# Moving the first weight block's operands beside the attention, with a fifth row buffer and earlier scores

## The chip, the cores and the metric

The kernel runs on one core of one Trainium2 chip. The metric is the time of one execution in device microseconds (us). The engines are named as the profile names them: PE (TensorE; PEld is its weight load), DVE (VectorE), ACT (ScalarE), POOL (GpSimd) and SP (SyncE, which here only issues DMAs).

## The reference

Two layers in float32. First a "talking heads" attention over 4 batches, 12 heads, 448 positions and 64 values per head: the heads are mixed with a 12x12 matrix before the softmax and with another after it. Then a gated layer on the 1792 rows of 768 values that come out.

```python
scores = scale * np.matmul(q, k.transpose(0, 1, 3, 2))
scores = np.einsum('bhij,hg->bgij', scores, w_pre)
scores = scores - np.max(scores, axis=-1, keepdims=True)
attn = np.exp(scores)
attn = attn / (np.sum(attn, axis=-1, keepdims=True) + 1e-09)
attn = np.einsum('bhij,hg->bgij', attn, w_post)
x = np.matmul(attn, v)          # then (1792, 768)
gate = 1.0 / (1.0 + np.exp(-(x @ w_gate)))
val = x @ w_val
return gate * val @ w_out       # w_gate, w_val (768, 1536), w_out (1536, 768)
```

## The kernel before, in words

**Attention.** The 448 query rows of a batch are cut into blocks of 120, 120, 120 and 88 rows, 16 blocks in all. A block is cut into units of twenty rows (two sets of ten; the last unit of a batch has one set): 6, 6, 6 and 5 units, 92 units in all (`NU`). One pass of the main loop is a slot `s`. In it stand, for different units, the steps of a software pipeline: `scores` (q times k for two heads, then `keep` copies both to the staging tile `st`, one copy on ACT and one on DVE), `regroup` (SP's DMA from `st` to a row buffer `T`, issued `LEAD` = 6 slots ahead of the slot that bears the unit's number, into `T` buffer u mod 4), `premix` (PE, three slots ahead, into three PSUM banks `pm` used in turn), `rowmax` (DVE, line 219), `expo` (ACT, 226), `norm` and `scale` (DVE reciprocal 232, POOL 238: `ph`, the high half of the probabilities), `p_lo` (DVE 244: the low half), `postmix` (PE 256), `mix` (ACT 264) and `av` (PE 285: times v, one block later; ACT evicts it, 293). The single tile of `postmix` is read by `mix` before the next `postmix` may write it.

**The gated layer.** Weights and x are held as a pair of f16 halves: `round` (ACT, 1147) makes the high half, `rest` (DVE, 1152) the low one. A product of 2x2 blocks is done with seven products instead of eight, so each block of weights (`w` 0 to 5) and each half of x (`x` 0 and 1) needs seven operand pairs, P1, P2, P6, P5, P7, P4, P3, made from four quarters and four sums or differences of them (DVE `tt`, 1161). A product step (`gate`, PE 1168) is 18 matmuls of 128x448. The first steps are P1 and P2 of `w` 0, P1 and P2 of `w` 1, then the other five of `w` 0. `out_mm` (1179) is the last layer.

**What sets the order.** The attention's order is the code of the loop and the table `plan`. The work of the gated layer is a list of tasks that a planner (`order_tasks`) sorts at build time by due times (`DUE`), by how long ahead a buffer may be taken (`AHEAD`, `LEAVE`) and by when room comes free (`ROOM`). `moe.slot` issues what the plan has up to a set of the attention: from 15 sets before its end on, that is from unit 84, `until` puts those tasks at the end of a slot, or, in the last seven slots, ahead of the slot's own `expo` and `p_lo`. So `w` 0's rounds, rests and sums stand on ACT and DVE among the last units and behind them. Eight weight tiles are converted earlier, beside the attention (`early`), in scratch space `raws`; the largest values of v, needed for x's scale, are summed by `v_sum` (ACT 179).

Of the kernel before, what the change touches and what calls it, by code (L numbers as in the profile page):

```python
# [41 lines left out]
def _attention(ctx, tc, ins, B, H, S, D, xs, raws, make_moe):  # L42
# [151 lines left out]
    t_bufs = [tp.tile([128, 2, S], F32, name=f"T{i}") for i in range(4)]  # L194
# [79 lines left out]
    def av(bi, c):  # L274
# [133 lines left out]
    for s in range(min(min(plan), -LEAD), max(plan) + 1):  # L408
# [43 lines left out]
        tail = (av, moe.between, moe.early)  # L452
# [19 lines left out]
        for fn, args in todo:  # L472
            if fn in tail:
# [27 lines left out]
class _Moe:  # L501
# [23 lines left out]
    DUE = {('raw', 2): -12.8, ('bound', 'w', 2): 72.0, ('w', 2): 20.3, ('raw', 3): -44.5, ('bound', 'w', 3): 106.5,  # L525
# [3 lines left out]
        ('store', 0): -57.0, ('keep_h', 0): -7.8, ('sum_of', 0): 125.4, ('sigmoid', 0): 22.8, ('hidden', 0): -7.6,  # L529
        ('copy', 0): -5.8, ('sum', 0): 54.2, ('load_x', 0): -59.0, 'raws': (120.6, 11.4), 'pairs': (127.3, 180.1)}  # L530
    ROOM = ((-15, dict(B=9, A=8)), (-7, dict(B=2, A=2, T=3)), (0, dict(B=3, A=5)), (9.6, dict(B=5, A=8, T=7, R=0)))
    AHEAD = {'raw': 194.1, 'half': 900.0, 'w': 900.0, 's': 95.9, 't': 99.5, 'wp': 900.0, 'wq': 8.0, 'q': 11.2, 'qp': 15.0,
        'c': 900.0, 'snap': 613.6, 'tmp': 686.1, 'wide': 95.9, 'hq': 157.8, 'hqp': 900.0, 'ow': 900.0, 'os': 33.0, 'owp': 39.1}

    def __init__(self, tc, xs, ins, out, raws, NG, top):
# [383 lines left out]
    def group(self, t):  # L919
# [9 lines left out]
        if t.fn in (self.load_w, self.round, self.rest, self.tt, self.keep_pair):  # L929
# [209 lines left out]
    def scales(self, by, n):  # L1139
        up = self.one[("up",) + by[1:]]  # L1140
        e = up.shape[1]
        return [(up[:, i:i + 1], slice(i * n // e, (i + 1) * n // e)) for i in range(e)]

    def round(self, pair, f, by):
        hi, f = self.f16(pair)[0], self.f32(f)
        for up, part in self.scales(by, f.shape[1]):
            self.nc.scalar.activation(out=hi[:, part], in_=f[:, part], func=AF.Copy, scale=up)  # L1147

    def rest(self, pair, f, by):
        (hi, lo), f = self.f16(pair), self.f32(f)  # L1150
        for up, part in self.scales(by, f.shape[1]):
# [162 lines left out]
```

## Time and profile before

| what | value |
|---|---|
| runs | 786.03, 786.04, 789.07 us; median 786.04 us |
| profiled execution, its own time | 784.43 us |
| its span, first to last instruction | 782.6 us |
| busy, share of span | PE 97%, DVE 81%, ACT 73%, POOL 33% |
| mean granted TensorE clock | 0.995 |

Busy shares are averages over two stages with different limits. Matmuls are pipelined and their ends are modelled, so the share of PE hides short waits. The attention stage lasts to about 340 us, the gated layer from about 342 us to the end. A duration in a row reaches past the start of the next instruction by some hundredths of a microsecond.

### The profile page before, as it was taken

What the parts mean: (1) busy time and instruction counts of PE and PEld (TensorE: products, weight loads), DVE (VectorE), ACT (ScalarE), POOL (GpSimd) and SP (SyncE); (2) the same over time, 40 slices, a digit from 0 to 9 for tenths busy, and PEclk for the clock granted to TensorE, in tenths of its full rate; (3) what the DMA queues carried; (4) which work ended last, traced back from release to release, by engine and by line L of the source; (5) the groups of instructions that cost most, each with busy time, mean ns of one, the idle gap of its engine ahead of it and who ended that gap; (6) DMA issues with size and microseconds to landing.
All of it is one profiled execution on the core that took longest, in us unless ns stands there. A gap on an engine that the chain in (4) does not pass through costs nothing.

```text
span 782.6 us, 23675 instructions
## 1 busy us (share of the span) xinstructions
PE 762.2 (97%) x9623; PEld 423.2 (54%) x9623; DVE 631.7 (81%) x1089; ACT 569.2 (73%) x1138; POOL 261.9 (33%) x429
## 2 busy tenths in 40 slices
PE   8999999999999999889999999999999999999998
PEld 2465666566556666564555555555555555555554
DVE  4988899889888998879997988588777999996111
ACT  4898999999899999876876876587756784562000
POOL 2564547454734455520322312234222221010000
PEclk9999999999999999989999999999999999999999
DMA  6786678758885574719407294654577788994001
GB/s 194 251 267 226 199 249 264 256 172 255 256 265 193 188 239 169 250 55 318 149 29 254 67 323 157 242 204 153 187 216 267 282 297 311 388 376 179 36 36 70
DMA packets 81117, 166.17 MB, mean 212 GB/s; under 512 B 20720, under 2 KB 58192, under 8 KB 81008
## 3 DMA queue, kind: packets, MB, share of 16 engines
q1 hardware_dynamic: 73006, 133.14, 51.7%
q0 software_dynamic: 7728, 31.27, 10.3%
q8 instruction: 75, 1.23, 0.7%
q14 instruction: 34, 0.28, 0.1%
q10 hardware_dynamic: 274, 0.25, 0.1%
HBM read 87.77 MB, written 38.15 MB: 161 GB/s over the span
## 4 chain that ended last, share of the span: by engine, by line
PE 83%; ACT 6%; DMA 5%; DVE 3%; issue 1%; POOL 1%; SPq 0%; ACTq 0%; DVEq 0%; POOLq 0%
PE bank L1168 34%; PE bank L1179 18%; PE pm L214 9%; PE av L285 8%; PE qk L160 7%; PE mx L256 6%; DMA T<-st 2%; ACT e L226 2%; ACT mix L264 1%; ACT m L1147 1%; DVE m L1152 1%; DMA q<-in_qp_dram 1%; ACT st L166 1%; DVE pl L244 1%; DMA m<-w 1%
## 5 line engine op out<-in xcount | busy, mean ns | idle before, releaser
L1168 PEld LDWEIGHTS <-m 128*128 128x128 f16 x1512 | 147.7, 98 | 140.1 <-DVE m L1152 2.1
L1168 PE MATMUL bank<-m,m 128*128 128x448 f16 x1116 | 214.2, 352 | 1.7 <-DVE m L1152 1.7
L238 POOL TENSOR_SCALAR ph<-e,ss 128x448 f16<-128x448 f32 x180 | 116.1, 654 | 142.6 <-DVE ss L232 97.9
L226 ACT ACTIVATE e<-pm,nm 128x448 f32<-128x448 f32 x177 | 113.5, 642 | 25.8 <-DVE nm L219 23.1
L219 DVE TENSOR_REDUCE nm<-pm 128x1 f32<-128x448 f32 x177 | 101.7, 615 | 27.4 <-PE pm L214 23.7
L244 DVE SCALAR_TENSOR_TENSOR pl<-e,ss,ph 128x448 f16<-128x448 f32 x180 | 115.6, 682 | 0.5 <-POOL ph L238 0.5
L1179 PEld LDWEIGHTS <-m 128*128 128x128 f16 x756 | 74.0, 98 | 69.0
L214 PE MATMUL pm<-T,w 64*64 64x448 f32 (+1 forms) x708 | 104.5, 560 | 2.8 <-DVE st L166 1.3
L264 ACT ACTIVATE mix<-mx 128x960 f32<-128x960 f32 (+1 forms) x92 | 104.5, 1136 | 1.6 <-PE mx L256 1.6
L256 PEld LDWEIGHTS <-ph 64*128 64x128 f16 x2880 | 63.7, 93 | 68.5 <-issue 39.6
L160 PE MATMUL qk<-k,q 64*64 64x448 f32 (+1 forms) x712 | 95.3, 539 | 1.6 <-ACT st L166 1.4
L1179 PE MATMUL bank<-m,m 128*128 128x448 f16 x468 | 92.9, 352 | 0.0
L285 PE MATMUL av<-mix,v 128*64 128x120 f32 (+1 forms) x1472 | 84.3, 268 | 2.2 <-issue 1.6
L1168 PE MATMUL bank<-m 128*128 128x448 f16 x396 | 77.9, 352 | 0.0
L285 PEld LDWEIGHTS av<-mix,v 128*64 128x64 f32 x1472 | 74.1, 140 | 5.1 <-issue 1.9
L256 PE MATMUL mx<-w2hi,ph 64*128 64x60 f16 x1440 | 71.7, 189 | 4.8 <-ACT mix L264 2.9
L256 PE MATMUL mx<-w2hi,pl 64*128 64x60 f16 x1440 | 70.4, 188 | 1.4 <-DVE pl L244 1.1
L1105 POOL CAST raws<-raws 128x768 f16<-128x768 bf16 x28 | 31.5, 1127 | 119.8 <-ACT raws L1099 119.8
L256 PE MATMUL mx<-w2lo,ph 64*128 64x60 f16 x1440 | 70.7, 187 | 0.0
L1099 ACT ACTIVATE raws<-raws 128x768 int16<-128x768 int8 (+1 forms) x72 | 60.2, 836 | 11.4 <-POOL raws L1105 11.2
L1195 DVE TENSOR_TENSOR m<-bank,m 128x448 f32<-128x448 f32 x72 | 44.6, 620 | 22.4 <-PE bank L1168 14.1
L256 PEld LDWEIGHTS <-pl 64*128 64x128 f16 x1440 | 61.1, 93 | 2.2 <-DVE pl L244 2.1
(134 smaller groups left out, 1080.2 us busy)
## 6 DMA issues: line engine op xcount, KB each, us to landing
T<-st SPq DMA_DIRECT2D x175, 210.0 KB
m<-w SPq DMA_DIRECT2D x60, 384.0 KB
raws<-in_w_dram SPq DMA_DIRECT2D x28, 767.6 KB
hs<-m POOLq DMA_DIRECT2D x48, 224.0 KB, 3.3
m<-hs SPq DMA_DIRECT2D x15, 672.0 KB
w<-m POOLq DMA_DIRECT2D x21, 384.0 KB, 4.9
w<-raws POOLq DMA_DIRECT2D x20, 384.0 KB, 4.7
v<-in_vb_dram SPq DMA_DIRECT2D x12, 512.0 KB
```

The source lines that it names most:

```text
L160: nc.tensor.matmul(sc[e][s0:s1, :S], lhsT=q[c][rows, s0:s1], rhs=k[rows, :], start=True, stop=True)
L214: nc.tensor.matmul(pm[bank][64 * x:64 * x + 64, :S], lhsT=w1[rows], rhs=T[rows, x], start=True, stop=True)
L219: nc.vector.tensor_reduce(nm[:, i:i + 1], pm[bank][:, :S], axis=AX.X, op=ALU.max, negate=True)
L226: nc.scalar.activation(out=e_t[u][:, i], in_=pm[units[u][2][i]][:, :S], func=AF.Exp, bias=nm_t[u][:, i:i + 1], scale=1.0, accum_out=ss_t[u ...
L238: nc.gpsimd.tensor_scalar(ph[:, i], e_t[u][:, i], ss_t[u][:, i:i + 1], 1.0, op0=ALU.mult, op1=ALU.mult)
L244: nc.vector.scalar_tensor_tensor(pl[:, i], e_t[u][:, i], ss_t[u][:, i:i + 1], p_t[u][0][:, i], op0=ALU.mult, op1=ALU.subtract)
L256: nc.tensor.matmul(mx[:, x, i, jb * HK:(jb + 1) * HK], lhsT=p[rows, i, JB[jb]:JB[jb] + 128], rhs=w[rows], start=(k == 0), stop=(k == 2))
L264: nc.scalar.activation(out=out.rearrange("p g (y r) -> p y g r", r=HALF), in_=mx_t.pop(u), func=AF.Copy, scale=1.0 / (P_UP * W_UP))
L285: nc.tensor.matmul(av_t[bi][64 * i:64 * i + 64, c % 2, :n], lhsT=vt[b, u][:, h + i, jb, :], rhs=mixes[bi % 2][:, jb, 2 * c + i, :n], start ...
L1099: self.nc.scalar.activation(out=out, in_=src, func=AF.Copy, scale=by)
L1168: self.nc.tensor.matmul(self.f32(bank), lhsT=w[a][:, k], rhs=x[b][:, k], start=self.START[i] and k == r == 0, stop=k == self.KH - 1 and r ...
L1179: self.nc.tensor.matmul(self.f32(bank), lhsT=w[a][:, k], rhs=b[bb], start=self.START[i] and j == k == r == 0, stop=j == OUT_TILES - 1 and ...
```

## The change

The seven operand pairs of `w` 0 are made by hand-placed calls (`first_w`) in slots `NU`-32 to `NU`-5, in `raws`, in halves of 384 columns for `round` and `rest`, and stored to DRAM by POOL's DMAs (`keep_pair`); the planner's list has seven `load_pair` tasks in their place. From slot `NU`-11 on the `rest` and `sum` calls stand right behind `rowmax` (`front`). Besides: five `T` buffers and `LEAD` 7, which issues `regroup` and `scores` one slot sooner; the `v_sum` of the last batch in slots `NU`-16 to `NU`-6; evictions of `av` in the last seven slots are put behind the second `expo`; and other numbers in the planner's tables.

```diff
-    t_bufs = [tp.tile([128, 2, S], F32, name=f"T{i}") for i in range(4)]
+    t_bufs = [tp.tile([128, 2, S], F32, name=f"T{i}") for i in range(5)]
...
-            if bi == NBK - 2 and c == KC - 1:
+            if NU - 7 <= s and bi < NBK - 1:
                 late.append(evict)
                 return
...
-    LEAD = 6
+    LEAD = 7
...
+    LAST_V = (-16, -14, -12, -10, -8, -6)
...
+            if b == B - 1:
+                s = NU + LAST_V[i]
             at(s, v_sum, b, i)
...
-            at(spread(c, NP, first[PB * (b - 1)] + 6, first[PB * b - 1] - LEAD - 2), k_load, b, c)
+            at(spread(c, NP, first[PB * (b - 1)] + 6, first[PB * b - 1] - LEAD - 1), k_load, b, c)
...
+    for slot, *args in moe.FIRST_W:
+        at(NU + slot, moe.first_w, *args)
...
+        front = [args for fn, args in todo if fn == moe.first_w and s >= NU - 11 and args[0] in ("rest", "sum")]
+        for args in front:
+            moe.first_w(*args)
...
-            elif s in (-4, -2):
+            elif s < -1 and (s + LEAD) % 2 == 0:
...
-            while late:
-                late.pop(0)()
...
         for e in ahead_u[1:]:
             expo(*e)
+        while late:
+            late.pop(0)()
...
+    FIRST_W = ((-32, "load", 0, 4), (-27, "load", 2, 0), (-26, "load", 3, 1), (-20, "load", 1, 3),
+               (-30, "round", 0, 4, 5), (-27, "round", 1, 4, 5), (-29, "rest", 0, 4, 5), (-26, "rest", 1, 4, 5), (-25, "keep", 0, 5),
...
-    ROOM = ((-15, dict(B=9, A=8)), (-7, dict(B=2, A=2, T=3)), (0, dict(B=3, A=5)), (9.6, dict(B=5, A=8, T=7, R=0)))
+    ROOM = ((-15, dict(B=9, A=7)), (-7, dict(B=2, A=2, T=3)), (0, dict(B=3, A=6)), (9.6, dict(B=5, A=8, T=7, R=0)))
...
-        ws = [self.operands(*(("w", 0, 4 * n + c) for c in range(4)), "w", (0, n), True, ("by", "w", n), 4 * n >= self.EARLY)
-              for n in range(FN)]
+        ws = [[("wp", 0, 0, i) for i in range(NP)]]
+        for i, pair in enumerate(ws[0]):
+            t = task(self.load_pair, dict(dma=1.1), ((pair, True),), pair, OUT_TILES, i)
+            t.ready = {P6: -26.0, P4: -18.0, P3: -11.0}.get(i, -1e9)
+        ws += [self.operands(*(("w", 0, 4 * n + c) for c in range(4)), "w", (0, n), True, ("by", "w", n), 4 * n >= self.EARLY)
+               for n in range(1, FN)]
...
+    def first_w(self, what, *args):
+
+        tiles = {("s", h): self.free["R"][h // 2][:, h % 2 * self.WE:(h % 2 + 1) * self.WE] for h in range(6)}
+        self.at.update(tiles)
+        if what == "load":
+            self.load_w(("s", args[1]), args[0])
+        elif what == "sum":
+            self.tt(*(("s", h) for h in args[:3]), args[3])
+        elif what == "keep":
+            self.keep_pair(("s", args[1]), OUT_TILES, args[0])
+        else:
+            e, f, pair = args
+            (self.round if what == "round" else self.rest)(("s", pair), ("s", f), ("by", "w", 0), e)
+        for name in tiles:
+            del self.at[name]
```

In the pieces of the order below, `one_w0` and `one_x0` are the scales of `w` 0 and of x's first half, so a SCALAR_TENSOR_TENSOR that reads one of them is a `rest` of that operand; `nm` is a `rowmax`, `ss` a reciprocal and `pl` a `p_lo`. The first is DVE among the last units, from the `nm` of unit 90 to the `pl` of unit 90, before:

```order
L219 TENSOR_REDUCE nm_8260<-pm1_116 128x1
L1161 TENSOR_TENSOR m_0_8080<-m_0_8080 128x768 x2
L244 SCALAR_TENSOR_TENSOR pl_8268<-e_8099,ss_8100,ph_8253 128x448 x2
L232 RECIPROCAL ss_8195<-ss_8195 128x2
L219 TENSOR_REDUCE nm_8349<-pm2_117 128x1
L1161 TENSOR_TENSOR m_0_8080<-m_0_8080 128x768
L244 SCALAR_TENSOR_TENSOR pl_8365<-e_8194,ss_8195,ph_8344 128x448 x2
L232 RECIPROCAL ss_8266<-ss_8266 128x2
L1152 SCALAR_TENSOR_TENSOR m_0_8080<-m_0_8080,one_w0_136 128x384 x2
L1152 SCALAR_TENSOR_TENSOR m_0_8080<-m_0_8080,one_x0_163 128x1344
L244 SCALAR_TENSOR_TENSOR pl_8429<-e_8265,ss_8266,ph_8420 128x448 x2
```

The same place on DVE now, from the `nm` of unit 90 on:

```order
L219 TENSOR_REDUCE nm_8296<-pm1_116 128x1
L244 SCALAR_TENSOR_TENSOR pl_8302<-e_8135,ss_8136,ph_8289 128x448 x2
L184 TENSOR_REDUCE vr_126<-vm_124 128x1
L185 TENSOR_SCALAR one_x1_164<-vr_126,wr_127 128x1
L1062 STREAM_TRANSPOSE junk_167<-one_x1_164 128x32
L232 RECIPROCAL ss_8228<-ss_8228 128x2
L219 TENSOR_REDUCE nm_8386<-pm2_117 128x1
L1201 SCALAR_TENSOR_TENSOR m_0_8116<-m_0_8116,one_x0_163 128x1344
L244 SCALAR_TENSOR_TENSOR pl_8402<-e_8227,ss_8228,ph_8381 128x448 x2
L232 RECIPROCAL ss_8300<-ss_8300 128x2
L1201 SCALAR_TENSOR_TENSOR m_0_8116<-m_0_8116,one_x0_163 128x1344
L244 SCALAR_TENSOR_TENSOR pl_8466<-e_8299,ss_8300,ph_8459 128x448 x2
```

The three sums and two rests of `w` 0 are gone from here; a rest of x stands where they stood, and three short instructions of the v bound. The second place is DVE in slot 82, before:

```order
L219 TENSOR_REDUCE nm_7848<-pm2_117 128x1
L219 TENSOR_REDUCE nm_7848<-pm0_115 128x1
L244 SCALAR_TENSOR_TENSOR pl_7854<-e_7682,ss_7683,ph_7841 128x448 x2
L232 RECIPROCAL ss_7757<-ss_7757 128x2
L219 TENSOR_REDUCE nm_7919<-pm1_116 128x1
```

and now, with the rests that `front` puts behind `rowmax`:

```order
L219 TENSOR_REDUCE nm_7877<-pm2_117 128x1
L219 TENSOR_REDUCE nm_7877<-pm0_115 128x1
L1201 SCALAR_TENSOR_TENSOR raws_63<-raws_63,one_w0_136 128x384 x2
L244 SCALAR_TENSOR_TENSOR pl_7885<-e_7714,ss_7715,ph_7870 128x448 x2
L232 RECIPROCAL ss_7788<-ss_7788 128x2
```

Two rests stand ahead of the `pl` that the next slot's `postmix` reads. The third place is DVE at the start of the gated layer, up to the second pair of `w` 1, before:

```order
L1152 SCALAR_TENSOR_TENSOR m_2_8620<-m_0_8080,one_w1_139,m_2_8620 128x384 x2
L1195 TENSOR_TENSOR m_3_8727<-bank3_8513,m_1_8355 128x448
L1161 TENSOR_TENSOR m_0_8080<-m_0_8080 128x1344
L1152 SCALAR_TENSOR_TENSOR m_2_8620<-m_0_8080,one_w0_136,m_2_8620 128x384 x4
L1044 TENSOR_REDUCE one_x1_164<-junk_167 128x1
L1152 SCALAR_TENSOR_TENSOR m_3_8727<-m_2_8620,one_w1_139,m_3_8727 128x384 x2
```

and now:

```order
L1201 SCALAR_TENSOR_TENSOR m_1_8392<-m_0_8116,one_x0_163,m_1_8392 128x1344
L1201 SCALAR_TENSOR_TENSOR m_2_8657<-m_0_8116,one_w1_139,m_2_8657 128x384 x2
L1201 SCALAR_TENSOR_TENSOR m_2_8657<-m_1_8392,one_w1_139,m_2_8657 128x384 x2
L1244 TENSOR_TENSOR m_3_8764<-bank2_8547,m_1_8392 128x448
```

The second pair of `w` 1 now follows the first at once; before, four rests of `w` 0 and a difference of x stood between them.

## Rows read from the trace of the kernel before

**Rows 1.** Chain that ended last, longest pieces: start us, us, what.

```profile
7.49 0.98 PE qk L160 x6
...
360.16 164.95 PE bank L1168 x871
...
635.99 143.02 PE bank L1179 x756
```

**Rows 2.** PE in order of time, 323 to 372 us: start, us, [idle before <-releaser].

```profile
323.88 1.86 PE L285 MATMUL av<-mix,v 128*64 128x120 f32 x32
...
331.89 3.16 PE L285 MATMUL av<-mix,v 128*64 128x120 f32 x32
...
349.76 1.43 PE L285 MATMUL mx<-mix,v 128*64 128x88 f32 x32 [0.90 <-ACT mix L293]
...
360.16 12.09 PE L1168 MATMUL bank<-m,m 128*128 128x448 f16 x63 [1.67 <-DVE m L1152]
```

**Rows 3.** Windows: stretch, its us, busy PE PEld DVE ACT POOL, clock, DMA.

```profile
242.00:318.00 76.00, 75.42 (x1794) 47.51 (x1791) 66.88 (x147) 69.41 (x163) 38.16 (x72) 1.00 0.58 193
318.00:340.00 22.00, 16.46 (x377) 11.99 (x374) 20.21 (x31) 17.80 (x31) 11.54 (x14) 0.88 0.72 229
340.00:360.00 20.00, 17.01 (x180) 10.94 (x176) 16.26 (x20) 15.93 (x26) 0.00 (x0) 0.96 0.37 111
```

**Rows 4.** DVE in order of time, 318 to 362 us.

```profile
321.12 1.14 DVE L1152 SCALAR_TENSOR_TENSOR m<-m,one_w 128x384 f16<-128x384 f32 x2
...
324.49 2.25 DVE L1161 TENSOR_TENSOR m<-m 128x768 f32<-128x768 f32 x2
...
328.44 1.18 DVE L1161 TENSOR_TENSOR m<-m 128x768 f32<-128x768 f32 x1
...
331.19 1.12 DVE L1152 SCALAR_TENSOR_TENSOR m<-m,one_w 128x384 f16<-128x384 f32 x2
...
357.18 2.20 DVE L1152 SCALAR_TENSOR_TENSOR m<-m,one_w,m 128x384 f16<-128x384 f32 x4
```

**Rows 5.** ACT in order of time: `mix` of units 82, 84, 85 and 91.

```profile
309.03 1.13 ACT L264 ACTIVATE mix<-mx 128x960 f32<-128x960 f32 x1
...
315.22 1.13 ACT L264 ACTIVATE mix<-mx 128x960 f32<-128x960 f32 x1
...
317.79 1.13 ACT L264 ACTIVATE mix<-mx 128x960 f32<-128x960 f32 x1
...
339.37 0.66 ACT L264 ACTIVATE mix<-mx 128x480 f32<-128x480 f32 x1 [0.46 <-PE mx L256]
```

**Rows 6.** ACT in order of time: `round` of `w` 0, and one that waited.

```profile
319.70 1.14 ACT L1147 ACTIVATE m<-m,one_w 128x384 f16<-128x384 f32 x2
...
356.64 1.12 ACT L1147 ACTIVATE m<-m,one_w 128x384 f16<-128x384 f32 x2 [1.57 <-DMA m<-w]
```

**Rows 7.** Windows in which DVE was fullest, was typical, and the clock fell.

```profile
322.00:332.00 10.00, 6.69 (x188) 4.76 (x184) 9.96 (x18) 8.95 (x17) 4.96 (x7) 0.96 0.87 272
...
160.00:200.00 40.00, 40.00 (x953) 24.91 (x948) 36.97 (x88) 37.01 (x88) 19.78 (x39) 1.00 0.72 224
...
330.00:334.00 4.00, 3.17 (x70) 3.08 (x71) 4.00 (x6) 3.14 (x3) 3.12 (x4) 0.65 0.80 257
```

**Rows 8.** Who waited for `T` and its DMA, in the view of tile `T`.

```profile
  DMA T<-st: 3.9, 7
```

**Rows 9.** Waits of PE, 40 to 240 us, and of PEld, 40 to 340 us: us, times, longest.

```profile
PE pm L214 <- DMA T<-st: 0.7, 1, 0.7
...
PEld L256 <- POOL ph L238: 20.8, 28, 1.8
```

**Rows 10.** POOL in order of time: a DMA issue, and `ph` of two units.

```profile
268.37 0.59 POOL L1117 DMA_DIRECT2D w<-raws  x1
...
323.69 1.25 POOL L238 TENSOR_SCALAR ph<-e,ss 128x448 f16<-128x448 f32 x2 [3.17 <-DVE ss L232]
...
331.44 3.21 POOL L238 TENSOR_SCALAR ph<-e,ss 128x448 f16<-128x448 f32 x2 [0.79 <-DVE ss L232]
```

More of the change, by code (lines that the diff above doesn't have):

```diff
@@ L451, in _attention @@
             p_lo(s + 1)
-        tail = (av, moe.between, moe.early)
+        tail = (av, moe.between, moe.early, moe.first_w)
         if s == NU - 1:
@@ L472, in _attention @@
         for fn, args in todo:
-            if fn in tail:
+            if fn in tail and args not in front:
                 fn(*args)
@@ L524 @@
     RAWS = 20.0
-    DUE = {('raw', 2): -12.8, ('bound', 'w', 2): 72.0, ('w', 2): 20.3, ('raw', 3): -44.5, ('bound', 'w', 3): 106.5,
[3 rows of a table removed]
-        ('store', 0): -57.0, ('keep_h', 0): -7.8, ('sum_of', 0): 125.4, ('sigmoid', 0): 22.8, ('hidden', 0): -7.6,
-        ('copy', 0): -5.8, ('sum', 0): 54.2, ('load_x', 0): -59.0, 'raws': (120.6, 11.4), 'pairs': (127.3, 180.1)}
-    ROOM = ((-15, dict(B=9, A=8)), (-7, dict(B=2, A=2, T=3)), (0, dict(B=3, A=5)), (9.6, dict(B=5, A=8, T=7, R=0)))
-    AHEAD = {'raw': 194.1, 'half': 900.0, 'w': 900.0, 's': 95.9, 't': 99.5, 'wp': 900.0, 'wq': 8.0, 'q': 11.2, 'qp': 15.0,
-        'c': 900.0, 'snap': 613.6, 'tmp': 686.1, 'wide': 95.9, 'hq': 157.8, 'hqp': 900.0, 'ow': 900.0, 'os': 33.0, 'owp': 39.1}
+    FIRST_W = ((-32, "load", 0, 4), (-27, "load", 2, 0), (-26, "load", 3, 1), (-20, "load", 1, 3),
+               (-30, "round", 0, 4, 5), (-27, "round", 1, 4, 5), (-29, "rest", 0, 4, 5), (-26, "rest", 1, 4, 5), (-25, "keep", 0, 5),
+               (-24, "sum", 4, 4, 0, ALU.subtract), (-23, "sum", 0, 0, 1, ALU.add),
+               (-22, "round", 0, 4, 5), (-21, "round", 1, 4, 5), (-21, "rest", 0, 4, 5), (-20, "rest", 1, 4, 5), (-19, "keep", 4, 5),
+               (-19, "sum", 4, 1, 4, ALU.subtract),
+               (-19, "round", 0, 0, 2), (-18, "round", 1, 0, 2), (-18, "rest", 0, 0, 2), (-17, "rest", 1, 0, 2), (-16, "keep", 3, 2),
+               (-17, "round", 0, 3, 5), (-15, "round", 1, 3, 5), (-16, "rest", 0, 3, 5), (-14, "rest", 1, 3, 5), (-13, "keep", 1, 5),
+               (-13, "sum", 3, 3, 4, ALU.subtract),
+               (-13, "round", 0, 4, 0), (-11, "round", 1, 4, 0), (-12, "rest", 0, 4, 0), (-10, "rest", 1, 4, 0), (-9, "keep", 2, 0),
+               (-11, "round", 0, 1, 2), (-9, "round", 1, 1, 2), (-10, "rest", 0, 1, 2), (-8, "rest", 1, 1, 2), (-7, "keep", 5, 2),
+               (-9, "round", 0, 3, 5), (-7, "round", 1, 3, 5), (-8, "rest", 0, 3, 5), (-6, "rest", 1, 3, 5), (-5, "keep", 6, 5))
@@ new lines @@
+    DUE = {('raw', 2): 12.3, ('bound', 'w', 2): 72.0, ('w', 2): 2.1, ('raw', 3): -44.5, ('bound', 'w', 3): 84.8, ('w',
+        3): -29.8, ('raw', 4): -107.6, ('bound', 'w', 4): 109.6, ('w', 4): -80.9, ('raw', 5): -334.4, ('bound', 'w',
+        5): -183.5, ('w', 5): -156.2, ('w', 1): -167.9, ('x', 1): -35.5, ('bound', 'h', 0): -397.8, ('h', 0): -480.7,
+        ('bound', 'h', 1): 181.5, ('h', 1): -2.8, ('load_h', 0): -79.5, ('load_pair', 0): -8.7, ('store', 0): -24.5,
+        ('keep_h', 0): -6.6, ('sum_of', 0): 134.9, ('sigmoid', 0): -0.7, ('hidden', 0): -7.6, ('copy', 0): 173.9,
+        ('sum', 0): 54.2, ('load_x', 0): -68.3, 'raws': (117.9, 13.8), 'pairs': (148.9, 161.6)}
@@ L632, in split @@
         more = 0.25 if by[1] == "w" else 0.07
-        self.task(self.round, dict(act=self.by_act(n)["act"] + more), ((f, False), (pair, True)) + uses, pair, f, by)
+        r = self.task(self.round, dict(act=self.by_act(n)["act"] + more), ((f, False), (pair, True)) + uses, pair, f, by)
         self.task(self.rest, dict(dve=self.by_dve(n)["dve"] + more), ((f, False), (pair, True)) + uses, pair, f, by)
+        if by == ("by", "x", 1):
+            r.ready = 24.0
     def combine(self, out, a, b, op=ALU.subtract):
@@ L936, in group @@
             return ("h", name[1][0]) if type(name[1]) is tuple else ("x", name[1])
+        if t.fn == self.load_pair and a[0][0] == "wp":
+            return "w", 0
         return t.fn.__name__, 0
@@ L1137, in load_h, with scales, round, rest @@
         self.nc.sync.dma_start(out=self.f32(name), in_=self.hs[p, u, j, t])
-    def scales(self, by, n):
+    def scales(self, by, n, part=None):
         up = self.one[("up",) + by[1:]]
         e = up.shape[1]
-        return [(up[:, i:i + 1], slice(i * n // e, (i + 1) * n // e)) for i in range(e)]
-    def round(self, pair, f, by):
+        return [(up[:, i:i + 1], slice(i * n // e, (i + 1) * n // e)) for i in range(e) if part in (None, i)]
+    def round(self, pair, f, by, e=None):
         hi, f = self.f16(pair)[0], self.f32(f)
-        for up, part in self.scales(by, f.shape[1]):
+        for up, part in self.scales(by, f.shape[1], e):
             self.nc.scalar.activation(out=hi[:, part], in_=f[:, part], func=AF.Copy, scale=up)
-    def rest(self, pair, f, by):
+    def rest(self, pair, f, by, e=None):
         (hi, lo), f = self.f16(pair), self.f32(f)
-        for up, part in self.scales(by, f.shape[1]):
+        for up, part in self.scales(by, f.shape[1], e):
             self.nc.vector.scalar_tensor_tensor(lo[:, part], f[:, part], up, hi[:, part], op0=ALU.mult, op1=ALU.subtract)
```

11 lines of the change are left out of this document (8 added, 3 removed), and 3 rows, old and new, of the table DUE.

## The prediction

> **What bounds the kernel now.** I read the chain that ended last first, then PE in order of time, then windows. In the chain [rows 1] the reader is to see two long unbroken runs of PE: from 360.16 us the gated layer goes on PE almost without a gap, the last piece starting at 635.99 and lasting 143.02, so that it ends at 779.01, and the span of 782.6 ends with one eviction and one store behind it. Whatever is done beside that run is worth nothing; the end moves only with the moment at which the run starts, and with any hole that is newly made in it. So the question is what happens before 360.16, and it has two parts. In PE's own order [rows 2] the run starts behind an idle time of 1.67 us that DVE's line 1152, a `rest`, ended; a shorter one, 0.90, stands at 349.76 for the eviction of the last values. In the windows [rows 3] three stretches differ: from 242 to 318 us PE is busy 75.42 of 76 us, with DVE at 66.88 and ACT at 69.41; from 318 to 340 PE falls to 16.46 of 22 while DVE has 20.21; from 340 to 360 PE has 17.01 of 20. So PE limits the attention up to 318, DVE its last units, and the handing over costs some microseconds more.
>
> **The change part by part.** All terms are made against the profiled execution, 784.43 us, of which 782.6 are span and 1.83 lie around it; the median of the runs shown, 786.04, is 1.61 above it, and I add the sum to the median.
>
> *The last units.* Between the `mix` of unit 85 at 317.79 and that of unit 91 at 339.37 [rows 5] lie 21.58 us for six units. Two units before them, without work of the gated layer between, took 315.22 - 309.03 = 6.19. On DVE the six carry two pieces of rests of `w` 0 (1.14 and 1.12) and sums of 2.25 and 1.18 [rows 4], 5.69 in all, and DVE is the engine that is full there. The order shows these gone; the rests of x stay, and one half rest of `w` 0 in unit 86 and the three short v-bound instructions come in. If the six units then go at 3.1 us each they take 18.6: a gain of 3.0. The bounds: nothing, if ACT, which keeps two long rounds of x there, takes DVE's place at once; and 6.5, if the 22.00 us shrink to ACT's own work, 17.80 less two pieces of 1.14 [rows 3, 6] = 15.5. I take 3.0, since the pace of 6.19 is seen right beside it.
>
> *The handing over.* PE's 1.67 us ends on the second pair of `w` 1. Ahead of that rest DVE did four rests of `w` 0 at 357.18, 2.20 us [rows 4], and ACT's round of `w` 1 at 356.64 had waited 1.57 for its load [rows 6]. Now both pairs of `w` 1 stand one behind the other, and the pairs of `w` 0 come by DMA. What is late next: ACT's chain of rounds of x and the last evictions, which stays, so the 0.90 stays too. I take -1.7; the bounds are nothing (if the load of `w` 1 is late all the same, behind the last stores on SP's queue) and 1.67 + 0.90 = 2.6.
>
> *What the attention takes in.* The 14 half rests, 14 half rounds and 4 sums are not gone, they stand in units 60 to 87; 13 rests, 13 rounds and all sums before unit 85, that is in the stretch of 242 to 318. On DVE: 66.88 + 13 x 0.57 + 4 x 1.13 = 78.8 us (0.57 is half of 1.14, 1.13 half of 2.25 [rows 3, 4]), on ACT: 69.41 + 13 x 0.57 = 76.8 [rows 3, 6], and the stretch took 76. So cover is gone: DVE, not PE, sets the pace there. With DVE entirely full the stretch takes 78.8, a loss of 2.8; if DVE fills only as it does at 160 to 200, 36.97 of 40 [rows 7], it takes 78.8 / 0.924 = 85.2, a loss of 9.2; the lower bound is no loss, and a gain is excluded since instructions are only added. Between them I take 2.8, since in the one window where rests and sums of this kind were the limit, 322 to 332, DVE was busy 9.96 of 10 [rows 7]. The two rests put ahead of a `pl` in slots 82 and 84 are in that figure. The seven stores cost POOL an issue of 0.59 each [rows 10], 4.1 us beside 38.16 of 76 [rows 3]: hidden, as long as POOL waits for DVE anyway. The loads are on SP, whose queue of stores is not waited for there; nothing.
>
> *Fifth buffer, `LEAD` 7.* A row buffer's DMA has one slot more to land. All waits for it sum to 3.9 us in seven times [rows 8], of which PE's own in the steady part is one of 0.7 [rows 9]. Against that one more pair of scores stands ahead of the first unit, as much as a piece of 0.98 in the chain [rows 1]. Bounds -3.9 and +1.0; I take -0.6, near PE's own wait. The later sums of v move six of ACT's steps a few slots on and the late evictions take one from between two `expo`: nothing, ACT being second to DVE there.
>
> *The planner's tables.* They reorder DVE, ACT and DMA work under the run of PE. The order of PE is the same instruction for instruction in the first steps of the layer, and I cost this at nothing; cover gone would cost the hole it makes.
>
> Sum: -3.0 - 1.7 + 2.8 - 0.6 = -2.5. The profiled execution would take 781.9, the median 783.5.
>
> **The rivals.** *The attention absorbs it (faster).* DVE idles 9 us of the 76, and if its backlog is hidden by the buffers the 2.8 goes to about 0.5; besides, PE's clock, 0.65 of full in 330 to 334 [rows 7], made the `av` there 3.16 where the one before took 1.86 [rows 2]. The fall followed PE's thin work in that stretch. With shorter holes one such loss, 1.3, falls away: -3.0 - 1.7 - 1.3 + 0.5 - 1.5 (half of the way to the bound for `T`) = -7.0, 779.0. For it speaks that PE has no wait in 242 to 318; against it that all three engines stand above 88% there.
>
> *DVE holds up POOL (slower).* Beside the two-operand work of DVE `ph` of one unit took 3.21 us, where it takes 1.25 otherwise [rows 10]: 1.96 more. PE's weight loads wait for `ph` 28 times, 20.8 us in all [rows 9]: it is often the last thing that `postmix` waits for. The change puts 17 such instructions in the stretch. Where one falls on a `ph` it costs up to 1.96; if it does so on five of them, 9.8 are lost in place of 2.8: -3.0 - 1.7 - 0.6 + 9.8 = +4.5, 790.5. Against it: most of them stand behind the `pl`, when POOL waits for the next reciprocal; only those of slots 82 and 84 stand where `ph` may run. It decides from four overlaps on: up to there the gains of 5.3 cover it to within a median's scatter. The Trainium skill ("SBUF — State Buffer", section "SBUF: two separate sides") calls the port that VectorE and GpSimd share an exclusive lock, taken by a VectorE operation with two SBUF inputs for the whole instruction. By that rule a `ph` would wait for a whole rest, 0.57, not for 1.96; the trace agrees that there is blocking (3.21 against 1.25), and by the rule's size 17 overlaps would be 9.7.
>
> *The gain goes elsewhere (no change).* Another operand is late at the handing over, say a round of x behind ACT's evictions, and the 1.7 and half of the 3.0 turn into that wait: -1.5 + 2.8 - 0.6 = +0.7, 786.7. For it: ACT is the chain there as soon as DVE is not, and x's long rounds stay.
>
> **How the numbers follow.** The forecast has a chance of 0.45, with a range of its own of 780 to 787; the faster case 0.28, the slower 0.12, no change 0.15. A measurement of this kernel can tell about 0.5% from no change, 3.9 us: below 782.1 is faster, above 790.0 slower. Of the forecast 0.13 lies below 782.1, of the slower case 0.10 above 790.0, of the last 0.01. That makes faster 0.41, same 0.48, slower 0.11. The range reaches from 777.5, somewhat below the faster case, to 789.0, short of the slower one; about 2 in 10 are left out.
>
> **What would show it.** Right: the long run of PE starts near 357.5 and without a wait for a rest; the `mix` of units 85 to 91 are some 3.1 us apart; DVE in the stretch before unit 85 is above 95% busy, and that stretch is 2 to 4 us longer. Wrong: a stretch as long as before (then the faster case), or one longer by 8 us with `ph` of 2 to 3 us in it (the slower one); a first run of PE that starts at 360 again behind a wait for ACT; or a hole in the run after 360, which would mean that the planner's tables cost something.

## The result, and the profile after

The changed kernel takes 793.02 us (median of four runs, 792.77 to 794.09), against 786.03 before: a ratio of 1.0083, with a 95% interval of 1.0055 to 1.0111, so 4.3 to 8.7 us slower. I had said 783.5, and 789.0 at most. The profiled execution of the changed kernel took 793.28 us, with a span of 791.5, against 784.43 and 782.6.

The chain that ended last, its longest pieces from the end of the attention on, answers to [rows 1]:

```profile
347.79 1.82 PE bank L1217 x9
350.17 1.31 ACT m L1196
351.88 1.46 PE av L285 x32
355.43 1.43 PE mx L285 x32
356.86 49.49 PE bank L1217 x261
...
414.86 1.64 DMA max_w<-junk
419.11 148.29 PE bank L1217 x783
...
581.69 5.55 DMA max_out<-junk
588.47 56.32 PE bank L1217 x288
644.79 143.02 PE bank L1228 x756
```

The long run of PE begins at 356.86, without the wait for a `rest` that stood there before, and where I had put it (near 357.5). But it is now three runs: it breaks off ahead of 419.11 and of 588.47, each time with a DMA of a small tile as the last thing waited for. PE in order of time at the two places:

```profile
414.69 3.57 PE L1217 MATMUL bank<-m 128*128 128x448 f16 x18
419.11 3.56 PE L1217 MATMUL bank<-m 128*128 128x448 f16 x18 [0.85 <-ACT m L1237]
...
588.47 5.25 PE L1217 MATMUL bank<-m 128*128 128x448 f16 x18 [2.35 <-ACT m L1237]
```

So an ACT copy out of PSUM (line 1237; the line numbers have moved by some fifty) held PE for 0.85 and 2.35 us. What held the copy is seen on ACT ahead of the second hole:

```profile
579.35 0.53 ACT L1237 COPY m<-bank 128x448 f32<-128x448 f32 x1 [1.17 <-PE bank L1217]
581.12 0.67 ACT L1247 ACTIVATE m<-m,back 128x448 f32<-128x448 f32 x1 [1.25 <-DVE back L1084]
587.33 0.58 ACT L1052 ACTIVATE junk<-m 128x448 f16<-128x448 f32 x1 [5.54 <-DMA max_out<-junk]
587.81 0.19 ACT L1052 ACTIVATION_READ_ACCUMULATOR junk<-m 128x1 f32 x1
587.90 0.51 ACT L1237 COPY m<-bank 128x448 f32<-128x448 f32 x1
```

Line 1052 is `sum_of`: ACT sums the magnitudes of a block, and its element-wise output is scrap, written into the tile `junk`. Other columns of the same tile hold the transposed maxima (`flip`), which a DMA takes to DRAM (`max_out<-junk`). The two touch no byte in common, but they are one tile, and waits are kept by tile: the sum waits until the DMA has landed, the copy is queued behind the sum, PE behind the copy. POOL, which issues that DMA, in order of time ahead of the second hole:

```profile
579.52 0.54 POOL L1166 DMA_DIRECT2D w<-raws  x1 [0.33 <-DVE raws L1162]
581.69 0.58 POOL L1067 DMA_DIRECT2D max_out<-junk  x1 [1.63 <-DVE junk L1062]
```

POOL waited 1.63 us for DVE's transpose before it issued the DMA, and the DMA then took 5.55 us to land (the chain above), where the one ahead of the first hole took 1.64. Stores of a converted weight tile had been issued just ahead of it; that they are what made it slow was not tried. Lateness alone is not the cause, either. In the kernel before, the same DMA took 4.6 us, and ACT's sum waited for it there too, but ACT's copies stood ahead of the sum:

```profile
581.64 0.51 ACT L1188 COPY m<-bank 128x448 f32<-128x448 f32 x1
583.25 0.63 ACT L1198 ACTIVATE m<-bank,back 128x448 f32<-128x448 f32 x1 [1.09 <-PE bank L1168]
586.40 0.58 ACT L1019 ACTIVATE junk<-m 128x448 f16<-128x448 f32 x1 [2.52 <-DMA max_out<-junk]
```

The second hole has one more cost. The 18 matmuls behind it took 5.25 us, where the 18 at 414.69 took 3.57: 1.68 more. The windows (stretch, its us, busy time of PE, PEld, DVE, ACT, POOL, clock, DMA share, GB/s) show the clock behind the first hole and behind the second:

```profile
419.10:422.60 3.50, 3.49 (x19) 1.84 (x19) 3.50 (x5) 3.10 (x7) 0.83 (x1) 1.00 0.92 322
589.30:592.70 3.40, 3.40 (x11) 1.38 (x10) 1.31 (x2) 2.08 (x5) 0.54 (x1) 0.50 0.79 252
```

Behind 2.35 us without work the granted clock was 0.50, that is 1.2 GHz in place of 2.4, for 3.4 us; behind 0.85 us it stayed at 1.00. From the start of the long run to the end of the span the changed kernel needs 434.7 us, and 429.5 in each of the six executions below in which the holes are mended: in the trace they cost 5.2.

For the attention, the starts of `mix` on ACT; units 60, 84, 85, 88 and 91 ([rows 5] has 84, 85 and 91 before):

```profile
240.67 1.15 ACT L264 ACTIVATE mix<-mx 128x960 f32<-128x960 f32 x1
...
322.98 1.15 ACT L264 ACTIVATE mix<-mx 128x960 f32<-128x960 f32 x1
...
326.17 1.14 ACT L264 ACTIVATE mix<-mx 128x960 f32<-128x960 f32 x1
...
337.46 1.15 ACT L264 ACTIVATE mix<-mx 128x960 f32<-128x960 f32 x1
...
347.16 0.63 ACT L264 ACTIVATE mix<-mx 128x480 f32<-128x480 f32 x1
```

Before, unit 60 started at 235.53. So from unit 60 to 85, the stretch up to which the prediction counts the intake, were 82.26 us and are 85.50: 3.24 more. From unit 85 to 91 were 21.58 and are 20.99: 0.59 less, of the 3.0 forecast. And unit 60 itself is 5.14 us late, long before the first weight block comes in. The stretch that I had taken for DVE's full one [rows 3]:

```profile
242.00:318.00 76.00, 75.09 (x1731) 45.02 (x1725) 73.50 (x155) 71.57 (x167) 44.82 (x72) 1.00 0.74 236
```

DVE 73.50 of 76 us, 96.7%, where it had 66.88.

### The profile page after: what moved, and what is told of

It reads as the page before. It is cut to its first block, busy times and chain, and to the rows that moved or that the text cites. A ratio compares the mean times of both kernels' runs of the same rounds, so it can differ in the third digit from the quotient of the medians.

```text
span 791.5 us, 23717 instructions
## 1 busy us (share of the span) xinstructions
PE 767.3 (97%) x9623; PEld 422.8 (53%) x9623; DVE 631.2 (80%) x1089; ACT 568.1 (72%) x1138; POOL 266.8 (34%) x437
## 3 DMA queue, kind: packets, MB, share of 16 engines
q8 instruction: 75, 1.23, 0.7%
## 4 chain that ended last, share of the span: by engine, by line
PE 81%; ACT 5%; DMA 5%; DVE 4%; issue 2%; POOL 2%; SPq 1%; ACTq 0%; POOLq 0%; DVEq 0%
PE bank L1217 32%; PE bank L1228 18%; PE pm L214 8%; PE av L285 8%; PE qk L160 7%; PE mx L256 6%; DMA T<-st 2%; ACT e L226 2%; ACT mix L264 2%; DMA m<-xs 1%; DVE nm L219 1%; DVE m L1201 1%; DVE pl L244 1%; DMA max_out<-junk 1%; ACT st L166 1%
## 5 line engine op out<-in xcount | busy, mean ns | idle before, releaser
L1217 PE MATMUL bank<-m,m 128*128 128x448 f16 x1116 | 213.2, 352 | 0.0
L238 POOL TENSOR_SCALAR ph<-e,ss 128x448 f16<-128x448 f32 x180 | 114.5, 646 | 140.6 <-DVE ss L232 84.8
L1228 PE MATMUL bank<-m,m 128*128 128x448 f16 x531 | 104.7, 352 | 0.0
L160 PE MATMUL qk<-k,q 64*64 64x448 f32 (+1 forms) x712 | 98.2, 540 | 4.3 <-ACT st L166 3.1
L1235 ACT ACTIVATE m<-bank,back 128x448 f32<-128x448 f32 x24 | 14.8, 632 | 71.0 <-PE bank L1228 71.0
L1237 ACT COPY m<-bank 128x448 f32<-128x448 f32 x72 | 37.8, 525 | 38.1 <-PE bank L1217 37.9
```

The lines of the kernel that those rows point to most:

```text
L160: nc.tensor.matmul(sc[e][s0:s1, :S], lhsT=q[c][rows, s0:s1], rhs=k[rows, :], start=True, stop=True)
L238: nc.gpsimd.tensor_scalar(ph[:, i], e_t[u][:, i], ss_t[u][:, i:i + 1], 1.0, op0=ALU.mult, op1=ALU.mult)
L1217: self.nc.tensor.matmul(self.f32(bank), lhsT=w[a][:, k], rhs=x[b][:, k], start=self.START[i] and k == r == 0, stop=k == self.KH - 1 and r ...
L1228: self.nc.tensor.matmul(self.f32(bank), lhsT=w[a][:, k], rhs=b[bb], start=self.START[i] and j == k == r == 0, stop=j == OUT_TILES - 1 and ...
```

## Experiments

Theories: (A) the sooner scores cost the 5 us by unit 60, in the slots that bear two scores jobs; (B) the shared scrap tile costs the two holes. Rivals: the rows and buffers cost it; the holes only move on; or what two traces differ by is chance. Where a diff is against the changed kernel, it says so.

**1. Scores alone** (before, scores seven slots ahead, rows still six, four buffers).

```diff
-    LEAD = 6
+    LEAD = 7
+    ROWS = 6
...
-        next_dma = rows_until(s + LEAD, next_dma)
+        next_dma = rows_until(s + ROWS, next_dma)
```

> The kernel before, with the scores of every round one slot sooner (lead 7 in place of 6) and nothing else: rows still six units ahead, four row buffers. Theory (the sooner scores cost the time, by slots that take two scores jobs without a product with the values beside them): about 5 us slower than before, 791 us, with the start of the mix of unit 13 some 3 us later than in the kernel before and that of unit 60 some 5 us later. Rival (the loss belongs to the row buffers or to the other parts of the change): 786 us, starts within 0.5 us of before.

Measured: 790.17 us, 1.003 of before (1.0001 to 1.0059). Unit 13 starts 2.3 and unit 60 4.3 us later than in the first trace of before, in the same steps as in the changed kernel: +1.3 at unit 12, +1.4 at 35, +1.5 at 58. Slower, but by half of what A said; and the step at unit 58 is not the pair's alone (see 5).

**2. The changed kernel with `LEAD` 6.** Since `rows_until` takes `LEAD` too, its rows stand six units ahead again; the expectation is wrong in saying that they stay at seven. Only the five buffers stay.

```diff
-    LEAD = 7
+    LEAD = 6
...
```

> The changed kernel with the scores put back to six slots ahead; five row buffers and rows seven units ahead stay, and so do the first block's operands and the late evictions. Theory (sooner scores cost 5.3 us by unit 60): 787.7 us, the mix of unit 60 starts within 0.5 us of the kernel before. Rival (fifth buffer and earlier rows cost it): 793 us, start of unit 60 still 5 us late.

Measured: 793.37 us, 1.0069 (1.0042 to 1.0095): as the changed kernel. The steps at units 12 and 35 are gone (0.0 and 0.4), that at 58 is not (1.5), and the time is not less. Theory A, as a sum, falls: something else that `LEAD` 7 had saved came back (see 4).

**3. The transferred columns in a tile of their own** (changed kernel; to make room, the maxima of `w` 4 and 5 share the place of 0 and 1).

```diff
...
-        both = top.tile([128, 288], F32, name="junk")
-        self.junk, self.flip = both[:, :256].bitcast(F16), both[:, 224:]
+        self.junk = top.tile([128, 256], F32, name="junk").bitcast(F16)
+        self.flip = top.tile([128, 64], F32, name="flip")
```

> The changed kernel with the columns that the transfer of the maxima reads (flip) in a tile of their own, apart from the scrap tile that ScalarE's sums write. Theory (ScalarE's sum waits for that transfer because both are one tile, the copy out of PSUM queues behind it and TensorE behind the copy): both holes of the gated layer go, at 418 us (0.85 us) and at 586 us (2.35 us), and the clock stays at 1.00 after 586 us; about 5 us less than after, 788 us. Rival (the holes come from ScalarE being late for another reason): 793 us, holes remain.

Measured: 787.45 us, 0.9992 (0.9971 to 1.0012). In its chain PE runs through, and ACT's sum, which had come at 587.33, comes at 581.45:

```profile
356.79 282.72 PE bank L1218 x1494
639.51 143.02 PE bank L1229 x756
```

```profile
581.45 0.58 ACT L1053 ACTIVATE junk<-m 128x448 f16<-128x448 f32 x1 [0.75 <-DVE m L1251]
```

No order of instructions differs, only what is one tile; the DMA of the maxima is as slow as before (issued at 580.6, 5.8 us to landing) and no longer holds anything. Theory B holds.

**4. Both 2 and 3.**

> The changed kernel with both: scores six slots ahead, and the transferred columns in a tile of their own. Theory (the two losses are independent and add): 793.0 - 5.3 - 5.0 = 782.7 us, faster than both kernels. Rival (one hides in the other or is a matter of where instructions lie): 787 to 788 us.

Measured: 787.73 us, 1.0002 (0.998 to 1.0023). Mending the holes is worth 793.37 - 787.73 = 5.64 us here, on one chip; in the trace of 2 PE waits 4.0 us in its two holes, here not at all. `LEAD` 6 against 7 makes +0.3 by the medians without the holes (787.73 and 787.45, on one chip); with them the ratios to before are 1.0069 and 1.0083, whose intervals overlap. The two do not add as A had it. What gives the gain of `LEAD` 6 back is seen in the traces of 4 and 3. At unit 60 the kernel with `LEAD` 6 is 2.4 us ahead (238.25 against 240.67); from 85 to 91 it takes 22.33 against 20.41, since ACT, ahead of unit 88, waits for the load of x that it rounds:

```profile
332.76 1.41 ACT L1197 ACTIVATE m<-m,one_x 128x1344 f16<-128x1344 f32 x1 [0.53 <-DMA m<-xs]
335.33 1.42 ACT L1197 ACTIVATE m<-m,one_x 128x1344 f16<-128x1344 f32 x1 [1.15 <-DMA m<-xs]
```

Experiment 2 has the same two waits (0.99 and 0.53); with `LEAD` 7 there are none. Why the load is later was not tried.

**5. and 6. Both kernels again, unchanged.**

> The kernel before, unchanged, in another execution: to see what is fixed in the program and what falls anew. If the stalls of TensorE that nothing in the trace releases (1.45 us at 210 us in the first execution) belong to the place in the program, it stands there again within 0.3 us; if they fall by chance, it is elsewhere or gone, and the starts of the mix of later units move by its size, 1 to 2 us.

> The changed kernel, unchanged, in another execution. Fixed place: stalls at 49.4 us (1.77) and 140.5 us (1.91) again, holes of the gated layer at 418 us and 586 us again. By chance: the stalls elsewhere, the holes of the gated layer (which follow from the order of the queues) still there. About 793 us either way.

Measured: 786.26 and 793.09 us. The second execution of before has unit 60 3.15 us later than its first; the changed kernel's second has it 5.20 late, as its first. So of the 5.14 us that I had laid to `LEAD`, some 3 lie within what one execution of the same program differs from another. The second execution of before also has a step at unit 58, 1.33, without any edit: there PE waits 1.04 us for `T`. The holes are at the same places (0.85 and 2.75 us), so they belong to the order. The stalls of PE with no releaser, all above 0.6 us in the attention, are these in the second execution of the changed kernel:

```profile
44.05 1.24 PE L285 MATMUL av<-mix,v 128*64 128x120 f32 x19 [1.08 <-issue]
...
128.77 0.20 PE L256 MATMUL mx<-w2hi,ph 64*128 64x60 f16 x2 [0.68 <-issue]
...
141.26 0.98 PE L285 MATMUL av<-mix,v 128*64 128x120 f32 x14 [0.79 <-issue]
...
227.72 0.20 PE L256 MATMUL mx<-w2hi,pl 64*128 64x60 f16 x2 [1.92 <-issue]
```

In the first they were two, 1.77 at 51.13 and 1.91 at 142.40. One is at the same instruction, the others are not: both answers of the expectation are half right (see the last section).

**7. The pairs of scores at the values** (3, and in the three slots that bear two jobs the second one moved to the next slot, which has an `av`).

```diff
-            at(spread(c, NP, s0, s1), scores, bi, c)
+            at(spread(c, NP, s0, s1) + (s1 - s0 < NP and c == 1), scores, bi, c)
```

> The changed kernel with the transferred columns in a tile of their own, and the slots that take two scores jobs (11, 34 and 57) moved on by one, to the slots with a product with the values. Theory (the second job's evictions fit beside that product, and hold up a slot without it by about 1.3 us each): the starts of the mix of units 12, 35 and 58 come 1.3, 1.3 and 1.4 us less late, in all 3 to 4 us less than with the transferred columns alone: 784 us. Rival (the place of the double slot does not matter; what is lost there is the rows' transfers or chance): 787.5 us.

Measured: 784.94 us, 0.997 of before (0.9948 to 0.9992). The steps at units 12, 35 and 58 are 0.0. ACT in order of time in the slot of unit 11 of the changed kernel, without an `av`, two jobs in it:

```profile
63.12 1.16 ACT L264 ACTIVATE mix<-mx 128x960 f32<-128x960 f32 x1
...
64.71 0.66 ACT L179 ACTIVATE v_abs<-v 128x512 bf16<-128x512 f32 x1
...
65.76 0.55 ACT L166 COPY st<-qk 120x448 f32<-120x448 f32 x1
...
67.38 0.53 ACT L166 COPY st<-qk 120x448 f32<-120x448 f32 x1 [0.44 <-PE qk L160]
68.15 1.15 ACT L264 ACTIVATE mix<-mx 128x960 f32<-128x960 f32 x1 [0.24 <-PE mx L256]
...
72.66 1.15 ACT L264 ACTIVATE mix<-mx 128x960 f32<-128x960 f32 x1
```

From unit 11 to 13 are 9.54 us; in the kernel with the pairs moved 8.47 (63.99 to 72.46), in the one before 8.49. ACT has next to no rest in that slot, and the second job's copy lengthens it; beside the 1.8 us of an `av` the same copy costs nothing. So the place of the pair is what costs, about 1 us each time. That is read from the starts of the units; the ratios of 3 and 7 (0.9992 and 0.997) have intervals that overlap.

**8. Rounds behind** (7, and the gated layer's work of the last seven slots issued behind the second `expo`).

```diff
-            gated()
...
-        if 0 <= s < NU and not soon:
+        if 0 <= s < NU:
             gated()
```

> As the kernel with the pairs moved, and in the last seven units the gated layer's work is issued behind the attention's own (the first exponential, the mix, the second exponential) instead of ahead of it. Theory (the two roundings of the first values tile on ScalarE, 2.74 us, ahead of an exponential and a mix hold up unit 88 by about 1.7 us): the start of unit 88 comes 4.8 to 3.1 us behind unit 87, the last mix about 1.5 us sooner, 782.5 us if the gated layer begins sooner by that much. Rival (those roundings are due before the gated layer's second block and what the attention gains is given back there): 784 us, same as with the pairs moved.

Measured: 787.69 us, 1.001 (0.9989 to 1.0032). Unit 88 starts 3.34 us behind 87 where it was 4.80, as the theory had it. But two waits of PE for `ph`, 1.52 and 1.72 us, come in its place, so that units 84 to 91 gain only 0.5 (23.91 against 24.39), and `mix` of unit 91 to the run of PE takes 357.51 - 345.66 = 11.85 us where 7 has 356.33 - 346.69 = 9.64. What the last units gain is given back at the handing over, as the rival had it, and more: the rival expected 784 us. Its reason is not seen, though. ACT's rounds are not late there, since ACT waits 2.61 us for PE at 350.35; but the `av` at 345.49 takes 3.01 us, at a granted clock of 0.50 from 341.1 to 347.9, where in 7 it takes 1.86.

**9. Scores alone, pairs moved** (1 with the edit of 7).

> The kernel before with the scores one slot sooner (as in the first experiment), but its three slots with two scores jobs moved on by one, to the slots with a product with the values. If the place of those slots is what the sooner scores cost: the step of about 1.3 us at the starts of units 12, 35 and 58 goes, and it takes about 3 us less than with the scores alone, 786 to 787 us, level with before. If the sooner scores are a gain of their own once the slots are right (and the gain of the kernel with the pairs moved comes from them): 783 to 784 us. If the place does not matter: 789 to 790 us.

Measured: 789.94 us, 1.0021 (1.0002 to 1.004), near what it was. The steps at units 12 and 58 are gone, that at 35 is down to 0.6; the gain isn't there. With rows six ahead PE still waits for `T`, here 9.8 us in all (PE and PEld, 19 to 345 us), 2.8 of them ahead of unit 0. The same view of the waits for `T` (who, in total us, times, longest) of the changed kernel, then of the second execution of before:

```profile
PEld pm L214 <- DMA T<-st: 1.6, 3, 0.8
```

```profile
PE pm L214 <- DMA T<-st: 1.7, 3, 1.0
PEld pm L214 <- DMA T<-st: 4.5, 8, 0.9
```

In seven executions with rows six ahead (experiments 1, 2, 4, 9, 11, before twice) PE and PEld wait 3.5 to 9.8 us for `T`, in seven with rows seven ahead and five buffers (the changed kernel twice, 3, 7, 8, 10, 12) 1.4 to 3.0. So experiments 2 and 4 saved the three pairs' 3 us and gave up two things for it: these shorter waits, and the 1.9 us in the units from 85 on. What the waits are worth in time of the kernel no run shows by itself, and none has rows seven ahead with four buffers.

**10. Sums on GpSimd** (7, and the four sums of `first_w` by POOL in place of DVE).

```diff
-            self.tt(*(("s", h) for h in args[:3]), args[3])
+            o, a, b = (self.f32(("s", h)) for h in args[:3])
+            self.nc.gpsimd.tensor_tensor(o, a, b, op=args[3])
```

> As the changed kernel with the transferred columns apart and the pairs moved, and the four sums of weight tiles that go beside the attention made by GpSimd, not by VectorE. Theory (the 2.6 to 3 us that units 69 to 84 lose are VectorE's, which is over 98% busy there): four sums of about 0.6 us leave it, the start of unit 84 comes 1 to 2 us sooner relative to unit 60, 783.5 us. Rival (GpSimd needs longer for such a sum and holds up its own scaling of the probabilities, or keeps VectorE waiting): no gain or 1 us slower, 785 to 786 us.

Measured: 788.75 us, 1.0013 (0.9994 to 1.0032), worse than 7. Units 60 to 84 take 6.3 us more than before, in 7 2.6. A sum, and beside it DVE's `pl`, which is 1.27 us elsewhere:

```profile
283.77 1.83 POOL L1127 TENSOR_TENSOR raws<-raws 128x768 f32<-128x768 f32 x1
```

```profile
283.30 3.40 DVE L244 SCALAR_TENSOR_TENSOR pl<-e,ss,ph 128x448 f16<-128x448 f32 x2
```

DVE does such a sum in 0.95 us. POOL's takes nearly twice that, and DVE's two `pl` take 3.40 - 1.27 = 2.13 longer beside it. The Trainium skill ("SBUF — State Buffer", section "SBUF: two separate sides") says that of a VectorE operation with two SBUF inputs and a GpSimd operation that reads SBUF, the one that starts first holds the shared port for its whole instruction, and the other is blocked. This trace agrees that one of the two stands still, here DVE; that the first to start wins it does not show, since the row of `pl` starts 0.47 us ahead of the sum's. Of the rival in the prediction, DVE holding up `ph`, the changed kernel shows little: the mean `ph` is 646 ns there, over 180 of them, and 654 before.

**11. Control: before with the columns apart.**

> Control: the kernel before with the transferred columns in a tile of their own. In the kernel before, ScalarE's sum waits for that transfer as well (3.6 us at 419 us) without TensorE stopping, so nothing should change: 786 us, within 1 us of before. If it gains 5 us here too, the gain in the changed kernel is not from the two holes.

Measured: 787.37 us, 0.9991 (0.9972 to 1.0011): no difference, so what 3 gained was the holes.

**12. Experiment 7 again.**

> The kernel with the transferred columns apart and the pairs moved (0.997 of before, interval 0.9948 to 0.9992), once more on the chip that this call gets, to see whether it is faster than before at all. If so: again 0.996 to 0.999 of before, with both holes of the gated layer and the steps at units 12, 35 and 58 absent. If the first time was chance: 1.000 or above. The stalls of TensorE that nothing releases, if they belong to its own stream of instructions, stand again at instruction numbers that are 193 more than a multiple of 256.

Measured: 785.2 us, 0.9971 (0.995 to 0.9992). It is faster than the kernel before by 0.3%, about 2.3 us, and than the changed kernel by about 1%. It is the fastest version found.

## Why the prediction was wrong

The step that failed is the planner's tables, put at nothing: the order that came of them costs 5.6 us. The last units were mis-sized as well. The terms, in the prediction's order, by what the runs showed:

*The last units: -3.0, measured -0.6.* It is -0.3 to -1.2 in the six executions with `first_w`, `LEAD` 7 and the rounds in their place. I let them go at 3.1 us as soon as DVE had lost the rests of `w` 0. The bound "nothing, if ACT, which keeps two long rounds of x there, takes DVE's place at once" is close to what came. ACT of the changed kernel, ahead of `mix` of unit 88:

```profile
334.24 2.74 ACT L1196 ACTIVATE m<-m,one_x 128x1344 f16<-128x1344 f32 x2
336.86 0.65 ACT L226 ACTIVATE e<-pm,nm 128x448 f32<-128x448 f32 x1
...
337.46 1.15 ACT L264 ACTIVATE mix<-mx 128x960 f32<-128x960 f32 x1
```

Before, one piece of `w` and one of x stood there, 1.14 + 1.43; now two of x, 2.74, since the planner filled the room that `w` left. Unit 88 starts 4.80 us behind unit 87 in the changed kernel, and 4.84 before. Putting these rounds behind gained nothing, as experiment 8 shows. The 3.1 us that I read beside it was the pace of units that hold no x work, and these hold it.

*The handing over: -1.7, measured -3.8 against the first execution of before, -2.3 against the second.* From `mix` of unit 91 to the run of PE that follows the last `av` were 11.76 us, with 1.67 of idle time in it behind [rows 2, 5]: 13.43; they are 9.63 now (347.16 to 356.79 in PE's order of time), with none. The 1.67 went as I said. Some 1.1 is the clock. The `av` behind the last `postmix` took 2.93 us in the trace of before and takes 1.86 now:

```profile
339.20 2.93 PE L285 MATMUL av<-mix,v 128*64 128x120 f32 x32
...
343.97 0.53 ACT L1188 COPY m<-bank 128x448 f32<-128x448 f32 x1 [1.97 <-PE bank L1168]
```

```profile
345.93 1.86 PE L285 MATMUL av<-mix,v 128*64 128x120 f32 x32
```

In that trace the granted clock was 0.50 (1.2 GHz) from 338.0 to 341.4 us, where PE had just waited 1.65 for `ph`. My step had no clock in it. In the second execution of before this `av` took 1.86 as well, and the handing over 10.29 + 1.67 = 11.96; in the other four executions without `first_w` it took 2.93 to 3.47, and in eight of the nine with it 1.86. ACT's four half rounds of `w` 0, 2.12 us at 339.88, are gone from here and were no cost: behind them ACT waited 1.97 us for PE. The last 1.1 only moves the border to the last units: `mix` of unit 91 starts 1.23 us behind that `av` now, and started 0.17 behind it. Together the two terms are -4.4, and -3.1 against the second execution, where I had -4.7.

*The attention's intake: +2.8, measured +3.2* (3.2 to 3.6 in the executions with `first_w` and without a stall in that stretch, but for experiment 10). DVE nearly full, as the step said.

*`LEAD` and the fifth buffer: -0.6, measured -0.3 within 2 us.* The net is right and its parts were not: I had one more pair of scores ahead of the first unit as the only cost. The cost is three slots where two jobs meet without an `av`, about 1 us each, against shorter waits for `T` and a load of x in time for unit 88. When the first two traces lay side by side, 5.14 us at unit 60 looked like `LEAD` alone; experiments 2, 4 and 5 took that back. The pairs are 2.8 of it, and PE's stalls without releaser 2.2 (3.68 us up to there, against 1.45).

*The planner's tables: nothing, measured +5.6.* "I cost this at nothing; cover gone would cost the hole it makes" was the step that failed, and the last of the signs of being wrong, a hole in the run after 360, is what came; none of the rivals had it. In the kernel before ACT's sum waited for such a transfer too, 3.64 us at 418.72 and 2.52 at 586.40, and no copy that PE needed stood behind it. The order of PE is unchanged in the layer's first steps, and from that I took the cover to be safe; what moved is the order on ACT and on POOL's queue of DMAs, which PE meets 60 and 230 us later. Which edit moved the sum ahead of the copy, the numbers of the tables or `w` 0's tasks gone from the list, no run separates. Of the 5.6, from experiments 2 and 4, the first trace shows 0.85 + 2.35 in the holes and 1.68 at the lower clock, 4.9, and 5.2 from the start of the run to the end.

The sum is -0.6 - 3.8 + 3.2 - 0.3 + 5.6 = +4.1, where 7.0 was measured (4.3 to 8.7). Without the holes it is -1.5, and experiment 3 measured 0.9992 of before, that is -2.3 to +0.9 us; so it is the holes that take the time out of the forecast's range, and what is left of the change is a smaller gain than the 2.5 forecast, or none. The two profiled executions differ by 8.9 us: 5.1 up to unit 60, 3.2 from there to unit 85, -4.4 from there to the long run, 4.9 in it. Between the sum and the measured 7.0 some 0.2 to 4.6 us are not settled. The stalls without releaser come to 1.5 to 2.1 us in five profiled executions without the change and 1.8 to 5.2 in nine with it; whether the change brings them, or chance, these runs can't tell. Of the rivals, none was the cause; the one in which DVE holds up POOL had the sign, and not the place. In the faster one the -1.5 for `T` is not half of the way from -0.6 to -3.9, which is -2.3; that changes nothing here.

## What to carry to other kernels

An unbroken run of the bound engine is cover for all that lies beside it only as long as nothing in a queue ahead of its own evictions can wait: before costing a reordering at nothing, list what stands ahead of each eviction and what that waits for. A scrap output and a buffer that a DMA reads belong in different tiles, even where their bytes don't meet. And two traces laid side by side show steps that belong to the program together with those that belong to the execution: run each program twice before laying a difference of 3 us to an edit.

## What the runs showed of the hardware that I had not expected

TensorE's stalls without releaser stand at fixed numbers of its instruction stream. I counted the trace's records of TensorE in order (weight loads, matmuls and its few semaphore instructions); eight of the stalls, in columns: kernel, stall from and to in us, number of the instruction that ends it, that number modulo 256, end of the last instruction packet that had landed before:

```
before         210.12-211.58   8897  193   209.91
before again   211.42-212.60   8897  193   211.19
after           49.36- 51.13   1473  193    49.58
after          140.49-142.40   5569  193   141.03
after again     42.97- 44.05   1217  193    42.49
after again    140.47-141.26   5569  193   139.94
after again    225.81-227.72   9409  193   226.24
pairs moved    226.25-227.88   9409  193   226.35
```

In fourteen executions 32 gaps above 0.6 us in the attention are marked so, and all are at 193 modulo 256; one more gap stands there that the profile puts down to a copy of DVE's, and none of the others. The page's list of DMA queues has the stream itself:

```profile
q8 instruction: 75, 1.23, 0.7%
```

75 packets, 16.4 KB each, for 19,246 weight loads and matmuls: about 257 instructions a packet. In the rows above a packet had landed 1.3 to 1.7 us before the stall ended. The Trainium skill ("Runtime: NRT & Kernel Launch", section "Instruction fetch mechanics") says that the instructions are brought in blocks of 256 over a DMA queue of the engine's own, and that the cost of crossing a block is mostly hidden. The trace agrees on the block; hidden it is not always: up to 2.55 us (experiment 3). In the stretches where such stalls came (40 to 52, 126 to 146 and 205 to 230 us) the largest data queue alone took 79% to 87% of the 16 DMA engines; that this makes a packet late was not tried. Which boundary is late changes from one execution to the next, and may be a part of why runs of one kernel on one chip lie up to 8 us apart (784.59 to 792.94 for the kernel before).
